# Falling output tiles sent whole to a row buffer in device memory and reversed there by later transfers

## The chip, the cores and the metric

The kernel runs on one core of a Trainium2 chip. The metric is device time in microseconds of one execution. Before the change it is 1046.65 us, the median of three runs (1045.64 to 1047.59).

The core has a matrix engine (TensorE, PE in the profile; PEld are its weight loads), a vector engine (VectorE, DVE), a scalar engine (ScalarE, ACT), a general engine (GpSimd, POOL) and a sync engine (SyncE, SP). Here SP issues nearly all transfers. Each engine takes its instructions in the order in which they were written and waits on semaphores for the others. 16 DMA engines carry the transfers.

## The reference

```python
# q, k, v: (4, 8, 768, 64); block 32
scores = q @ k.T / sqrt(64)                      # per batch and head
mask = neighbours | first, last block row/column | 3 sampled blocks per block row
attn = softmax(where(mask, scores, -1e9))
x = (attn @ v) heads side by side                # (4, 768, 512)
mixed = real(fft(fft(x, axis=1), axis=2))
u = x + mixed
un = (u - mean(u)) / sqrt(var(u) + 1e-6)
out = u + maximum(un @ w_ch1, 0) @ w_ch2         # 512 -> 2048 -> 512
```

## The kernel before

**Tiles.** The 768 rows (tokens) of a batch lie in six tiles of 128 partitions, three in `xA` (tiles 0, 1, 2) and three in `xB` (tiles 3, 4, 5), each 512 columns of 4 bytes, so a row is 2 KB. The order of rows in the tiles is not that of the tensor: it is chosen so that the Fourier transform can fold row s with row 768 - s. `_ORDER` (L53) lists it as (tile, first partition, runs, jump between runs, rows of a run, first row, step). In tiles 0, 1 and 5 the rows rise in steps of 2. In tiles 2, 3 and 4 they **fall** in steps of 2: partition 0 holds one row, partitions 1 to 63 and 64 to 126 two falling runs that interleave in the tensor, and partition 127 the last row. `_rows` (L81) turns this into access patterns; for a falling tile that is one transfer of one row, one of 126 rows (runs of 63, outermost dimension 2) and one of one row.

**Stages.** `slot` (L1566) is the attention for two units of 128 keys x 384 queries x 2 heads; there are 96 slots, 24 to a batch. In a slot PE makes scores (L583), ScalarE takes their exponential (L603, or L611 in place), VectorE applies the mask (L613), GpSimd or VectorE adds up (L643, L638), and PE multiplies by the values (L657). The scores go to one of two buffers of PSUM, so PE's next scores wait until L613 or L603 has read the ones before. Two heads' output is transposed (L680) and copied by ScalarE into `x` (`place`, L681), or, for later pairs, reaches `x` through a row buffer in device memory (`place_blocks`, L696 and L700).

When a batch's attention is done, its `mixer` runs in the gaps of the next batch's slots: the Fourier transform (`fourier`), normalization (L946 to L960), a block transpose (L1019) written to a buffer `far` (L1020), read back as `unT` (L1032, four loads of 192 KB for each half), differences of unT (L1070), the hidden layer by a scheme with seven products for eight (`quad`, L1116, sums L1121, relu L1125), and the output layer (`channels`, L1281; L1284 adds it into `x`). After the last of four rounds `channels` calls `store`, tile by tile: xA's in the order 2, 0, 1, then xB's 3, 4, 5.

**What sets the order.** All is written out ahead by a planner in Python that keeps a clock for each engine (`when`) and puts mixer steps (`apart`, `late`) into gaps (`gap`, `until`). Transfers have no place in its clocks: SP issues them in the written order. `x` has two buffers for each half, so batch b + 2 writes over batch b. `slot` therefore runs the rest of batch b's mixer (`until`, L1629 and L1644) before it places the first pair of batch b + 2, and the copy L681 waits for the transfers that read the old `x`. The last batch (`last`) has its own output scheme (`outputs`, L1349, L1356) with stores in halves.

Of the kernel before, what the change touches and what calls it, by code (L numbers as in the profile page):

```python
# [11 lines left out]
FP32 = mybir.dt.float32  # L12
# [10 lines left out]
def _words(ap, n):  # L23

    return bass.DRamTensorHandle(ap.tensor.name, (2 * n,), I32)
# [15 lines left out]
def _grid(ap, start, runs, jump, n, step):  # L41
# [17 lines left out]


_TURNED = (((0, 0, (128, 64, 2), (64, 128, 2), (1, 1, 64)),
# [19 lines left out]
def _rows(view, tile):  # L81

    got = []
    for t, p0, runs, jump, n, s0, step in _ORDER:
        if t != tile:
            continue
        at = view[s0:s0 + 1, :]
        row, col = list(at.ap[0])[0], list(at.ap[1])
        if jump > 0 > step:
            got.append((p0, runs * n, bass.AP(tensor=at.tensor, offset=at.offset,  # L90
                                              ap=[[jump * row, runs], [step * row, n], col])))
            continue
        for r in range(runs):
            at = view[s0 + r * jump:s0 + r * jump + 1, :]
            got.append((p0 + r * n, n, bass.AP(tensor=at.tensor, offset=at.offset,
                                               ap=[[step * row, n], col])))
    return got
# [3 lines left out]
def kernel(  # L101
# [14 lines left out]
    nc = tc.nc  # L116

    B, H, S, D = q.shape
    DM = H * D
    FF = w_ch1.shape[1]  # L120
    P = 128
# [9 lines left out]
    T = C // 2  # L131
# [55 lines left out]
    far_p = ctx.enter_context(tc.tile_pool(name="far_p", bufs=1, space=bass.MemoryType.DRAM))  # L187
# [114 lines left out]
    def bit(n):  # L302
# [5 lines left out]
                      in_=bass.AP(tensor=_words(sampled_blocks, NB * NR), offset=0,  # L308
                                  ap=[[0, NB], [1, 2 * NB * NR]]))
# [138 lines left out]
    for w, w_sb in ((w_ch1, w1_sb), (w_ch2, w2_sb)):  # L448
        rows, cols = w.shape
        words = _words(w, rows * cols)  # L450
        for row in range(rows // P):
            for col in range(0, cols, WN):
                src = bass.AP(tensor=words, offset=2 * (row * P * cols + col),
                              ap=[[2 * cols, P], [1, 2 * WN]])
# [527 lines left out]
    z_at = [0.0, 0.0]  # L982
    rstd_at = deque()
    finished = set()
    folded = set()

    def mixer(b, xA, xB):
# [56 lines left out]
        t, s = {}, {}  # L1044
# [243 lines left out]

        def store(half, m, cols=slice(0, DM), queue=nc.sync):
            x = (xA, xB)[half]  # L1290
            for p0, cnt, rows in _rows(out[b][:, cols], T * half + m):
                queue.dma_start(out=rows, in_=x[p0:p0 + cnt, m, cols])
            if cols.stop == DM:
                stored[half] += 1
            if stored[half] == T:
                finished.add((b, half))

        stored = [0, 0]
        last = b == B - 1
# [127 lines left out]
        for r in range(0 if last else NF // 4):  # L1430
# [21 lines left out]
    needed = set()  # L1452
    state = {"paired": False, "total": None, "w": 0, "got": 0, "owed": 0.0, "ready": 0.0,
             "back": 0.0, "place": None,
             "alone": False, "drain": lambda: None}

    def channel_step():
        masks["by_pe"] = False
        late.popleft()[0]()
# [61 lines left out]
    def until(met, alone=False):  # L1521

        state["alone"] = alone
        while not met():
            if late:
                channel_step()
                soon = state.pop("soon", None)
                gap(2.0, start=soon)
            else:
                do_apart()  # L1530
        state["alone"] = False
# [24 lines left out]
    def w_loads():  # L1556
        while state["got"] < min(len(wchunks), state["w"] + len(W_ROOMS)):
            w_load(state["got"])
            state["got"] += 1

    def w_steps(sl):
        while state["w"] < min(len(wchunks), W_PACE * sl):
            w_round(state["w"])
            state["w"] += 1

    def slot(sl):  # L1566
        phase, r = divmod(sl, SB)
        n, s = divmod(sl, SP)
        units = range(SLOT * sl, SLOT * sl + SLOT)
# [55 lines left out]
        if s >= ((4 if late else 5) if reuse else 3) and (n, 0) in oT_at and once(n):  # L1625
            b, j = pairs[n]
            at = oT_at[n, 0]
# [12 lines left out]
        if sl < B * SB and n % NP == 1 and s == 1:  # L1640
            b = pairs[n - 1][0]
            at = oT_at[n - 1, 1]
            if b >= 2:
                until(lambda: (b - 2, 1) in finished)  # L1644
                at = when["PE"] + LEAVES
# [46 lines left out]
        while short and (not more or soon) and (  # L1692
# [5 lines left out]
            short.remove(item)  # L1698
            item[2]()
        w_loads()  # L1700
        w_steps(sl)
        table_step(sl)

# [32 lines left out]
    begin(B - 1)  # L1736
    state["drain"] = lambda: None
    until(lambda: len(finished) == 2 * B, True)
    ordered.close()

    def general():
        qA = tp_p.tile([P, S], FP32, tag="qT", name="qA")
        kA = tp_p.tile([P, S], FP32, tag="kT", name="kA")
        spread_q(qA[D:KA, :], maskT)
        spread_k(kA[D:KA, :], ident[0:NB, 0:NB])
        for b in range(B):
            xs = [xp.tile([P, T, DM], FP32, tag=tag, name="x") for tag in ("xA", "xB")]
            for h in range(H):  # L1750
                qt = ld.tile([P, C, 2, D], FP32, tag="q", name="qg")
                for t in range(C):
                    for p0, cnt, rows in _rows(q[b, h], t):
                        nc.sync.dma_start(out=qt[p0:p0 + cnt, t, 0, :], in_=rows)
                nc.sync.dma_start(out=qt[:, :, 1, :],
                                  in_=k[b, h].rearrange("(p c) d -> p c d", p=P))
                vt = ldv.tile([P, C, D], FP32, tag="v", name="vg")
                nc.sync.dma_start(out=vt, in_=v[b, h].rearrange("(p c) d -> p c d", p=P))
                for half in range(2):
                    tp = ps_t.tile([P, HS], FP32, tag="t", name="tpg")  # L1760
                    for c in range(3):
                        nc.tensor.transpose(tp[:, c * P:(c + 1) * P],
                                            qt[:, 3 * half + c, :, :], ident)
                    sl = slice(half * HS, (half + 1) * HS)
                    nc.vector.tensor_scalar(out=qA[0:D, sl], in0=tp[0:D, :], scalar1=scale,
                                            scalar2=None, op0=ALU.mult)
                    nc.vector.tensor_copy(out=kA[0:D, sl], in_=tp[D:2 * D, :])
                op = ps_o.tile([P, C, D], FP32, tag="o", name="og")
                rs = sm.tile([P, C, 1], FP32, tag="r", name="rs", bufs=2)
                for t in range(C):  # L1770
                    s = ps_s.tile([P, 2, 512], FP32, tag="s", name="sg")
                    for half in range(2):
                        nc.tensor.matmul(s[:, half, 0:HS], qA[0:KA, t * P:(t + 1) * P],
                                         kA[0:KA, half * HS:(half + 1) * HS],
                                         start=True, stop=True)
                    nm = sm.tile([P, 1], FP32, tag="nm", name="nm")
                    nc.vector.tensor_reduce(out=nm, in_=s[:, :, 0:HS], axis=AX.XY, op=ALU.max,
                                            negate=True)
                    e = ep.tile([P, 2, HS], FP32, tag="e", name="eg")
                    nc.scalar.activation(out=e, in_=s[:, :, 0:HS], func=ACT.Exp, bias=nm,  # L1780
                                         scale=1.0, accum_out=rs[:, t, :])
                    eT = ep.tile([P, C, P], FP32, tag="e", name="eT")
                    for half in range(2):
                        tp = ps_t.tile([P, 3, P], FP32, tag="t", name="etp")
                        for c in range(3):
                            nc.tensor.transpose(tp[:, c, :], e[:, half, c * P:(c + 1) * P],
                                                ident)
                        nc.vector.tensor_copy(out=eT[:, 3 * half:3 * half + 3, :], in_=tp)
                    for c in range(C):
                        nc.tensor.matmul(op[:, t, :], eT[:, c, :], vt[:, c, :],  # L1790
                                         start=(c == 0), stop=(c == C - 1))
                nc.vector.tensor_scalar(out=rs, in0=rs, scalar1=1e-9, scalar2=None, op0=ALU.add)
                nc.vector.reciprocal(out=rs, in_=rs)
                for half, x in enumerate(xs):
                    sl = slice(half * T, half * T + T)
                    nc.vector.tensor_tensor(out=x[:, :, h * D:(h + 1) * D], in0=op[:, sl, :],
                                            in1=rs[:, sl, :].broadcast_to([P, T, D]),
                                            op=ALU.mult)
            before, after, rest = mixer(b, *xs)
            for step in before + after:  # L1800
                step[1]()
            for fn, _ in rest:
                fn()

    with tc.If(over > 0):
        general()
# [37 lines left out]
```

## Time and profile before

| | |
|---|---|
| median of three runs | 1046.65 us |
| the profiled execution | 1045.29 us |
| its span, first to last instruction | 1043.6 us |
| granted TensorE clock, mean | 0.994 |
| DMA | 58.06 MB, mean 56 GB/s |
| packets | 163582, of these under 512 B 144298 |
| output stores | 75 transfers, 71 from SP and 4 from ScalarE |

The busy time of an engine is its share of the span; transfers are counted by queue. In a timeline row stand the start and the duration in us, the engine, the line of the kernel, the operation, the tile written and the tile read, how many instructions were merged into the row, and in brackets how long the engine had been idle and what ended that. A waits row gives the total, the number and the longest of one kind of wait. "SPq" is SP's queue of issues; a duration there is the time to issue, not the time to land.

### The profile page before, as it was taken

The numbers are of one execution on the slowest core, as the hardware profiler recorded it, in microseconds if no ns is written. First come the engines' busy times: TensorE is split into PE (matmuls) and PEld (weight loads), VectorE is DVE, ScalarE is ACT, GpSimd is POOL, SyncE is SP. The second block draws the span as 40 slices with busy tenths as digits, with TensorE's granted clock in tenths as the row PEclk, the third lists the DMA queues.
The fourth block names the chain that finished last, engine by engine and source line by source line (L and its number), as shares of the span: only waits on it lengthen the run. The fifth ranks groups of instructions, "written<-read, shape, count | busy, mean of one in ns | idle before, by whom it ended". The sixth has DMA issues, their size and how long they took to land.

```text
span 1043.6 us, 12498 instructions
## 1 busy us (share of the span) xinstructions
PE 1018.6 (98%) x4382; PEld 537.0 (51%) x4382; DVE 683.2 (65%) x1246; ACT 359.3 (34%) x727; POOL 257.7 (25%) x287
## 2 busy tenths in 40 slices
PE   8999999999999999999999998999999999999996
PEld 4444345435565454444535653444444764578575
DVE  6899895978745646655677367665458475674663
ACT  6998765563021012433341111253220221210210
POOL 1000173662000203545560003256540221000000
PEclk9999999999999999999999999899999999999998
DMA  7767422291000143322320005521010001000001
GB/s 213 225 190 234 99 47 46 51 153 25 1 1 20 41 58 65 73 47 45 63 46 1 1 20 101 91 48 43 17 23 8 0 1 42 20 0 1 1 19 45
DMA packets 163582, 58.06 MB, mean 56 GB/s; under 512 B 144298, under 2 KB 154296, under 8 KB 163512
## 3 DMA queue, kind: packets, MB, share of 16 engines
q1 hardware_dynamic: 162216, 56.46, 24.1%
q10 hardware_dynamic: 1264, 0.72, 0.3%
q8 instruction: 36, 0.59, 0.2%
q14 instruction: 34, 0.28, 0.1%
q0 software_dynamic: 32, 0.01, 0.0%
HBM read 43.80 MB, written 13.37 MB: 55 GB/s over the span
## 4 chain that ended last, share of the span: by engine, by line
PE 84%; DVE 8%; DMA 2%; ACT 2%; SPq 2%; issue 1%; ACTq 0%; DVEq 0%
PE y L1281 20%; PE z L1116 16%; PE s L583 11%; PE o L657 9%; PE yp L1116 8%; PE yy L1349 7%; PE xp L1116 4%; PE zp L865 2%; PE sp L728 1%; PE s L593 1%; DMA far<-un 1%; ACT e L603 1%; DVE t L1070 1%; PE yz L1224 1%; DVE acc L638 1%
## 5 line engine op out<-in xcount | busy, mean ns | idle before, releaser
L643 POOL TENSOR_TENSOR acc<-acc,e 128x384 f32<-128x384 f32 x160 | 163.4, 1054 | 126.3 <-DVE e L613 106.7
L583 PE MATMUL s<-qT,kT 64*128 64x384 f32 x768 | 154.5, 518 | 9.5 <-DVE e L613 5.4
L657 PE MATMUL o<-e,vr 128*64 128x384 f32 x768 | 141.7, 497 | 0.0
L1281 PE MATMUL y<-w_sb,hB 128*128 128x512 f32 x264 | 118.9, 601 | 0.0
L1281 PE MATMUL y<-w_sb,hA 128*128 128x512 f32 x264 | 117.1, 595 | 0.0
L613 DVE TENSOR_TENSOR e<-s,mask 128x768 f32<-128x768 f32 x86 | 78.3, 950 | 53.9 <-ACT s L611 45.9
L583 PEld LDWEIGHTS s<-qT,kT 64*128 64x128 f32 x768 | 64.4, 187 | 90.0 <-ACT e L603 22.7
L1284 DVE TENSOR_TENSOR x<-y,x 128x512 f32<-128x512 f32 x66 | 45.6, 691 | 98.3 <-PE y L1281 98.1
L611 ACT ACTIVATE s<-s 128x768 f32<-128x768 f32 x86 | 65.1, 791 | 107.3 <-PE s L583 107.2
L603 ACT ACTIVATE e<-s 128x768 f32<-128x768 f32 x106 | 81.0, 814 | 54.2 <-PE s L593 32.9
L643 POOL TENSOR_TENSOR acc<-e 128x384 f32<-128x384 f32 x42 | 48.7, 1180 | 201.5 <-ACT e L603 121.9
L1116 PE MATMUL z<-unT,t 128*128 128x384 f32 x256 | 93.1, 486 | 0.0
L657 PEld LDWEIGHTS o<-e,vr 128*64 128x64 f32 x768 | 47.9, 136 | 69.4 <-issue 67.0
L1281 PEld LDWEIGHTS y<-w_sb,hB 128*128 128x128 f32 x264 | 49.6, 192 | 62.0 <-issue 61.3
L1121 DVE TENSOR_TENSOR hA<-z,hA 128x384 f32<-128x384 f32 x64 | 35.7, 557 | 69.8 <-PE z L1116 69.7
L1281 PEld LDWEIGHTS y<-w_sb,hA 128*128 128x128 f32 x264 | 49.2, 190 | 59.5 <-issue 55.7
L1125 ACT ACTIVATE hA<-hA 128x384 f32<-128x384 f32 x64 | 33.5, 523 | 121.8 <-DVE hA L1121 121.8
L1116 PEld LDWEIGHTS z<-unT,t 128*128 128x128 f32 x256 | 48.6, 190 | 34.1 <-DVE hA L1121 0.4
L1125 ACT ACTIVATE hB<-hB 128x384 f32<-128x384 f32 x64 | 33.5, 523 | 86.0 <-DVE hB L1121 86.0
L1136 ACT COPY hA<-xp 128x384 f32<-128x384 f32 x32 | 15.3, 477 | 129.3 <-PE xp L1116 129.3
L1116 PE MATMUL z<-t,w_sb 128*128 128x384 f32 x128 | 46.7, 487 | 1.5 <-DVE t L1070 1.5
L1116 PE MATMUL xp<-unT,w_sb 128*128 128x384 f32 x128 | 47.2, 492 | 0.0
(236 smaller groups left out, 1440.4 us busy)
## 6 DMA issues: line engine op xcount, KB each, us to landing
wraw<-in_moe_w_ch_dram SPq DMA_DIRECT2D x32, 512.0 KB
vr<-in_v_dram SPq DMA_DIRECT2D x30, 192.0 KB
far<-un SPq DMA_DIRECT2D x18, 256.0 KB
unT<-far SPq DMA_DIRECT2D x24, 192.0 KB
qb<-in_q_dram SPq DMA_DIRECT2D x44, 96.0 KB
kb<-in_k_dram SPq DMA_DIRECT2D x44, 96.0 KB
out_dram<-x SPq DMA_DIRECT2D x11, 252.0 KB
out_dram<-x SPq DMA_DIRECT2D x19, 128.0 KB
```

The costliest lines, as they stand in the source:

```text
L583: nc.tensor.matmul(s[:, i, 0:HS], kT[rows, c * P:(c + 1) * P], qT[rows, queries], start=True, stop=u not in by_pe)
L603: nc.scalar.activation(out=e, in_=s[:, :, 0:HS], func=ACT.Exp, scale=scale)
L611: nc.scalar.activation(out=s[:, :, 0:HS], in_=s[:, :, 0:HS], func=ACT.Exp, scale=scale)
L613: nc.vector.tensor_tensor(out=e, in0=s[:, :, 0:HS], in1=m.broadcast_to([P, 2, HS]), op=ALU.mult)
L643: nc.gpsimd.tensor_add(out=acc[:, i, :], in0=start[:, i, :], in1=e[:, i, :])
L657: nc.tensor.matmul(o[D * i:D * i + D, :], vt[:, i, c, :], e[:, i, :], start=(c == 0), stop=(c == C - 1))
L1116: nc.tensor.matmul(to, a[:, k, :], c[:, k, :], start=(k == 0), stop=(k == ND // 2 - 1))
L1121: tt(out=to, in0=ps, in1=a, op=ALU.add)
L1125: nc.scalar.activation(out=h, in_=h, func=ACT.Relu)
L1281: nc.tensor.matmul(y, hs[0, half][:, l, m * P:(m + 1) * P], w2_sb[:, 4 * r + l, :], start=(l == 0), stop=(l == 3))
L1284: nc.vector.tensor_tensor(out=x[:, m, :], in0=y, in1=x[:, m, :], op=ALU.add)
L1349: nc.tensor.matmul(ps, a[:, k, :], c[k // 2][:, k % 2, :] if isinstance(c, list) else c[:, k, :], start=(k == 0), stop=(k == 3))
```

## The change

A falling tile of the first three batches is sent whole, 128 rows as they lie, to a buffer of device memory (`falls`, two buffers for each of the three tiles). For tiles 2 and 3 the store of partition 0's row stays as it was. The other rows are put in a list, `owed`, as two transfers for each tile, from the buffer to `out`: 63 or 64 falling rows each (64 rows for both of tile 4, whose first row joins its first run). Such a transfer has sixteen column parts of 32 elements (128 bytes) as its outermost dimension, then the rows. At the end of each slot, ahead of `w_steps`, one of them is issued if it comes from an earlier slot. What is left is issued ahead of the last batch's first store. The last batch's own stores are not changed. The written order of PE, ScalarE, VectorE and GpSimd has no part in it.

```diff
+_FALLS = {2: ((1, 63, 382), (64, 64, 383)), 3: ((1, 63, 766), (64, 64, 767)),
+          4: ((0, 64, 640), (64, 64, 639))}
...
         def store(half, m, cols=slice(0, DM), queue=nc.sync):
             x = (xA, xB)[half]
+            while owed and last:
+                owed.popleft()[1]()
+            falls = T * half + m in _FALLS and not last
+            if falls:
+                turn_round(T * half + m, x[:, m, :])
             for p0, cnt, rows in _rows(out[b][:, cols], T * half + m):
-                queue.dma_start(out=rows, in_=x[p0:p0 + cnt, m, cols])
+                if not falls or (p0 == 0 and _FALLS[T * half + m][0][0]):
+                    queue.dma_start(out=rows, in_=x[p0:p0 + cnt, m, cols])
...
+        def turn_round(t, x):
+
+            rows = far_p.tile([P, DM], FP32, tag=f"fall{t}", name="falls", bufs=2)
+            nc.sync.dma_start(out=rows, in_=x)
+
+            def fall(p0, n, s0):
+                at, to = rows[p0:p0 + 1, :], out[b][s0:s0 + 1, :]
+                w = DM // 16
+                nc.sync.dma_start(
+                    out=bass.AP(tensor=to.tensor, offset=to.offset,
+                                ap=[[w, 16], [-2 * DM, n], [1, w]]),
+                    in_=bass.AP(tensor=at.tensor, offset=at.offset,
+                                ap=[[w, 16], [DM, n], [1, w]]))
+
+            for run in _FALLS[t]:
+                owed.append((state["slot"], lambda run=run: fall(*run)))
...
     def slot(sl):
+        state["slot"] = sl
...
         w_loads()
+        if owed and owed[0][0] < sl:
+            owed.popleft()[1]()
         w_steps(sl)
```

More of the change, by code (lines that the diff above doesn't have):

```diff
@@ L984 @@
     finished = set()
+    owed = deque()
     folded = set()
@@ L1454 @@
              "back": 0.0, "place": None,
-             "alone": False, "drain": lambda: None}
+             "slot": 0, "alone": False, "drain": lambda: None}
     def channel_step():
@@ L1738 @@
     until(lambda: len(finished) == 2 * B, True)
+    assert not owed
     ordered.close()
@@ L1803, in general @@
                 fn()
+            while owed:
+                owed.popleft()[1]()
     with tc.If(over > 0):
```

## The prediction

> **What bounds the kernel now.** I read the page first, then the waits, then the timeline around the one long stop of TensorE, then the granted clock in short windows.
>
> ```profile
> span 1043.6 us, 12498 instructions
> PE 1018.6 (98%) x4382; PEld 537.0 (51%) x4382; DVE 683.2 (65%) x1246; ACT 359.3 (34%) x727; POOL 257.7 (25%) x287
> ACT x L681 <- DMA far<-un: 8.7, 1, 8.7
> ACT x L681 <- DMA out_dram<-x: 1.9, 1, 1.9
> PE s L583 <- DVE e L613: 5.4, 2, 4.5
> ```
>
> TensorE (PE) is busy for 98% of the span, so a change in transfers can give only what PE idles (25 us in all) or what the clock loses. The third column of a wait is the longest one: a single copy on ScalarE, the placing of attention output into x (L681), waits 8.7 us for a transfer, and PE waits once for 4.5 us. The timeline shows that these are one event, in the fourth batch's attention (us from the start, duration; "x" counts merged instructions, the bracket is idle time before):
>
> ```profile
> 633.06 1.53 SPq L1292 DMA_DIRECT2D out_dram<-x  x3
> 635.09 0.35 SPq L1020 DMA_DIRECT2D far<-un  x1
> 636.49 1.19 SPq L1292 DMA_DIRECT2D out_dram<-x  x2
> 637.79 0.53 SPq L1020 DMA_DIRECT2D far<-un  x1
> 641.98 3.96 SPq L1032 DMA_DIRECT2D unT<-far  x4
> 645.98 1.94 SPq L1292 DMA_DIRECT2D out_dram<-x  x2
> ...
> 646.00 2.80 PE L657 MATMUL o<-e,vr 128*64 128x384 f32 x16
> ...
> 650.26 0.48 ACT L681 COPY x<-xt 128x384 f32<-128x384 f32 x1 [8.70 <-DMA far<-un]
> 650.64 0.85 ACT L540 ACTIVATE kb<-kb 128x768 f32<-128x768 f32 x1
> ...
> 651.48 1.50 ACT L611 ACTIVATE s<-s 128x768 f32<-128x768 f32 x2
> 652.31 1.82 DVE L613 TENSOR_TENSOR e<-s,mask 128x768 f32<-128x768 f32 x2 [3.91 <-ACT s L611]
> ...
> 653.32 2.93 PE L583 MATMUL s<-qT,kT 64*128 64x384 f32 x8 [4.52 <-DVE e L613]
> ...
> 656.18 5.15 PE L1281 MATMUL y<-w_sb,hB 128*128 128x512 f32 x8
> ```
>
> L681 overwrites the x of the second batch, so it waits for that batch's three xA stores (633.06, 636.49, 645.98). The profile names far<-un, but L681 touches no such tile; queue semaphores are shared, and the last store is the transfer that ends there. Behind L681 on ScalarE stand the exponentials (L611), behind them the masks (L613), and PE's next scores need the bank that L613 frees: 3.06 us from L681 to PE (650.26 to 653.32). PE ran dry at 648.80 and stood 4.52 us.
>
> Why was the last store issued only at 645.98? SP issues in order, and the four unT<-far loads before it waited until 641.98 for far<-un. The first two of these rows of the chain of waits price that transfer (the third is for a rival below):
>
> ```profile
> 635.09 6.83 DMA far<-un
> 648.66 2.59 DMA far<-un
> ...
> 662.76 3.63 DMA kb<-in_k_dram
> ```
>
> The same 256 KB took 6.83 us from issue to landing just behind the store of tile 2, and 2.59 us elsewhere. That store is the falling one: 126 rows as two runs of 63 in one transfer.
>
> ```profile
> 637.00:641.00 4.00, 4.00 (x18) 1.72 (x17) 3.18 (x6) 0.94 (x2) 0.77 (x2) 1.00 0.82 217
> 641.00:643.00 2.00, 2.00 (x7) 0.93 (x6) 1.04 (x3) 0.56 (x1) 0.00 (x0) 1.00 0.12 47
> ...
> 660.00:660.90 0.90, 0.90 (x4) 0.27 (x2) 0.00 (x0) 0.00 (x0) 0.00 (x0) 1.00 0.13 36
> ```
>
> The last three columns are granted clock, busy share of the 16 DMA engines, and GB/s. A share of 0.12 to 0.13 is two engines of sixteen; it follows each falling store (tile 2 here, tile 3 at 660). At 36 to 47 GB/s, 252 KB take 5.5 to 7.2 us, and whatever is spread over all engines lands only after those two.
>
> **The change, part by part.**
>
> *Removed:* nine falling stores (tiles 2, 3, 4 of three batches) and their last-row stores. *Added in their place:* one whole-tile transfer, x to a row buffer, with the shape of far<-un: 256 KB, priced at 2.59 us to landing and 0.35 to 0.53 us of SP, against 1.53 us for the three issues now. Tile 4's first-row store goes too. L681 and all later users of x then wait for this transfer and not for the reversal.
>
> *The gain at 633 to 656.* With far<-un landing 2.59 us after 635.09, that is at 637.68, SP is held only by its own issue until 637.79 + 0.53 = 638.32. The unT<-far loads then start at 638.32 and not 641.98, **3.66 us** sooner, and the xA store behind them likewise. That is the upper end. The lower end: the engines were 0.82 busy from 637 to 641, and this load stays, so the unT pieces may not move before 641.0; they now move from 643.0 at the earliest (the window up to there has only the two engines), so at least **2.0 us** are gained. The waiting time at the engines is shorter than this, since far<-un itself starts sooner; I take **3.0 us**, between the ends, nearer to the issue rows that SP's order gives directly. L681 then runs at 647.3, PE resumes at 650.3, and 1.5 of the 4.52 us stay.
>
> *The clock.* After the stop PE's instructions are long: 2.93 us for eight score matmuls and 5.15 us for a y, against these:
>
> ```profile
> 644.51 1.56 PE L583 MATMUL s<-qT,kT 64*128 64x384 f32 x8
> ...
> 640.98 3.60 PE L1281 MATMUL y<-w_sb,hB 128*128 128x512 f32 x8
> ...
> 529.40:530.30 0.90, 0.07 (x1) 0.00 (x0) 0.90 (x2) 0.49 (x1) 0.16 (x1) 1.00 0.57 91
> ...
> 649.00:653.30 4.30, 0.00 (x0) 0.00 (x0) 0.99 (x2) 3.04 (x6) 0.00 (x0) 0.89 0.48 157
> 653.30:656.00 2.70, 2.68 (x8) 1.14 (x8) 0.91 (x2) 1.68 (x4) 0.00 (x0) 0.50 1.28 166
> ```
>
> Excess: (2.93 - 1.56) + (5.15 - 3.60) = 1.37 + 1.55 = **2.92 us**. In 649.0 to 653.3 the clock averages 0.89; at half clock that is 4.3 x 0.11 / 0.5 = 0.95 us, so it fell at 652.35, 3.55 us into the idleness. The stop of 0.83 us before 530.3 left it at 1.00. A rest of 1.5 us, or 2.5 at the lower end, should keep it full. So the whole 2.92 us go.
>
> *Sum at this place:* 3.0 + 2.92 = 5.9 us; bounds 2.0 + 2.92 = 4.9 and 4.52 + 2.92 = 7.4 (no rest at all).
>
> *What is late next.* The right-hand differences, before which PE stops again:
>
> ```profile
> 665.79 0.69 DVE L1284 TENSOR_TENSOR x<-y,x 128x512 f32<-128x512 f32 x1 [2.99 <-PE y L1281]
> 666.39 1.42 DVE L1070 TENSOR_TENSOR t<-unT 128x768 f32<-128x768 f32 x1
> 667.85 1.64 DVE L1070 TENSOR_TENSOR t<-unT,t 128x768 f32<-128x768 f32 x1
> ...
> 669.63 1.53 PE L1116 MATMUL z<-t,w_sb 128*128 128x384 f32 x4 [1.30 <-DVE t L1070]
> ```
>
> L1070 has no idle before it: VectorE comes from L1284, which waits for PE. This 1.30 us stop follows PE's own order and shifts with it; I cost it at nothing. After it PE is the bound (98% of the span), so the shift reaches the end.
>
> *The first batch's stores (390 to 418)* delay L681 there by 1.9 us. PE's waits of this kind (scores for L613) come to 5.4 us, 4.5 of them in the stop above; so at most 0.9 us can be had here. I take 0, since PE had other products queued. *The third batch's* x is not reused: nothing.
>
> *The reversals:* 18 transfers, memory to memory, 126 or 128 KB each in 128-byte pieces, one per later slot. The trace has none. Nearest rows:
>
> ```profile
> 655.00:657.00 2.00, 2.00 (x5) 0.60 (x4) 0.96 (x1) 1.50 (x2) 0.00 (x0) 0.50 1.44 140
> ...
> 433.30 2.63 SPq L696 DMA_DIRECT2D row<-oT  x4
> 437.52 2.50 SPq L700 DMA_DIRECT2D x<-row  x4
> ...
> 657.82 6.89 SPq L232 DMA_DIRECT2D kb<-in_k_dram  x4
> ...
> 691.56 2.29 SPq L232 DMA_DIRECT2D kb<-in_k_dram  x4
> L681 ACT COPY x<-xt x20: 472/479/570, 26.1 to 682.9; 128x384 f32<-128x384 f32 x20
> SPq L1292 <- DVE x L1356: 137.2, 6, 121.9
> ```
>
> Lower end: 128-byte reads at 140 GB/s, 128 KB in 0.9 us. Upper end: 192 KB of row<-oT, 128-byte writes to memory, were issued and landed by 437.52, 4.2 us, so 2.8 us a reversal. I take 2 us, with about 0.6 us of SP each (row<-oT: 2.63 / 4). In SP's order the first stands behind the second batch's tile 3 store, the second behind the four kb loads, the other four behind the vr loads; none precedes anything of the sum above. They delay kb, the xB stores and vr by at most 5.6 us, while the kb loads, 6.89 us now behind a clogged pair of engines and 2.29 elsewhere, give 4.6 back. The xB placing (the last L681, 682.9) comes 12 us after the last xB store lands (664.81 + 3.34 + 2.6 = 670.7). Slack covers them: cost 0, and without that cover 5.6 us. The third batch's six are flushed in the order ahead of the last batch's first store, so SP issues them at once after that batch's stores, in its 121.9 us of idleness.
>
> [...]
>
> **Rivals.**
> 1. *The wait moves to L1070.* In the chain of waits a kb load lands at 666.4 (662.76 + 3.63), just where L1070 starts; L1070 reads unT and not kb, so the name may again stand for a shared semaphore. If unT's second half really lands only then, it moves 3.0 us sooner with SP's order, while PE comes 5.9 sooner: 2.9 us are lost again, gain 3.0, **1043.7 us**. Against: no idle before L1070.
> 2. *Half of the way.* Only 0.9 us or less is gained because another transfer holds unT<-far; PE still rests over 3.55 us and the clock falls: **1045.8 us**.
> 3. *It doesn't do what it says:* the buffer transfer also runs on few engines, or L681 waits for the row as before: **1046.7 us**. Against: far<-un has its shape.
> 4. *Slower: the reversals clog.* Two stand in SP's order ahead of the last xB stores. These have 12 + 4.6 = 16.6 us of slack to L681. From 8.3 us each on, L681 waits again and PE with it, 1 us for 1 us, and beyond 3.55 us the clock falls. At 14 us each: 28 - 16.6 = 11.4 us of stop and 2.9 of clock, less 5.9: **1055 us**. Against: five times the row<-oT price.
>
> **How the numbers follow.** The profiled execution took 1045.29 us (1043.6 and 1.7 around it); the median shown is 1046.65, 1.36 above. 1045.29 - 5.9 = 1039.4 on the one scale, **1040.7 us** on the other. Its own range, 4.9 to 7.4 us of gain and 1 us of scatter of the shown runs, is 1038.2 to 1042.8. Chances: forecast 0.66, rival 1 0.11, rival 2 0.06, rival 3 0.06, rival 4 0.11. The range 1037.6 to 1046.0 leaves out rival 4 and most of rival 3. A measurement can tell 0.2% (2.1 us) from no change: faster 0.77, same 0.12, slower 0.11.
>
> **What would show it.** Right: L681 near 647 with an idle of about 5 us or less before it; PE's stop before the scores under 2.5 us; clock 1.00 right after; kb's four issues near 2.3 us; no window at share 0.13. Wrong: L681 still near 650; a stop before L1070 or a later L681; windows in which reversals hold all engines for over 5 us.

## The result, and the profile after the change

The changed kernel takes 1041.90 us, the median of eight runs (1040.81 to 1043.65), and the kernel before 1045.77 us in eight runs beside it (1044.88 to 1047.59). The ratio is 0.9961, 95% interval 0.995 to 0.9972: **faster by 3.9 us**, and the interval stays clear of no change. The forecast was 1040.7 us and a gain of 5.9 us. The profiled execution took 1040.81 us, the shortest of the eight; its span is 1039.0 us, its mean granted clock 0.998.

The same views as before, in the same order. First the page's head and two rows of the waits (total, number, longest):

```profile
span 1039.0 us, 12502 instructions
PE 1016.1 (98%) x4382; PEld 536.0 (52%) x4382; DVE 683.2 (66%) x1246; ACT 359.4 (35%) x727; POOL 257.8 (25%) x287
ACT x L685 <- DMA far<-un: 5.8, 1, 5.8
PE s L587 <- DVE e L617: 2.4, 2, 1.6
```

The placing into x (L681 before, now L685) waits 5.8 us and not 8.7, and PE's longest wait for scores is 1.6 us and not 4.5. PE has the same 4382 matmuls with 2.5 us less busy time: work that ran at half clock before. The timeline of the same place in the changed kernel:

```profile
633.20 0.32 SPq L1315 DMA_DIRECT2D falls<-x  x1
635.23 0.32 SPq L1025 DMA_DIRECT2D far<-un  x1
...
638.59 4.13 SPq L1037 DMA_DIRECT2D unT<-far  x4
642.77 2.03 SPq L1303 DMA_DIRECT2D out_dram<-x  x2
647.46 0.48 ACT L685 COPY x<-xt 128x384 f32<-128x384 f32 x1 [5.75 <-DMA far<-un]
650.52 1.78 PE L587 MATMUL s<-qT,kT 64*128 64x384 f32 x8 [1.58 <-DVE e L617]
652.23 3.70 PE L1286 MATMUL y<-w_sb,hB 128*128 128x512 f32 x8
655.07 2.72 SPq L236 DMA_DIRECT2D kb<-in_k_dram  x4
663.93 2.18 SPq L1320 DMA_DIRECT2D out_dram<-falls  x3
664.22 1.53 PE L1121 MATMUL z<-t,w_sb 128*128 128x384 f32 x4 [1.30 <-DVE t L1075]
```

Read it against the rows of before. The buffer transfer (L1315) is one issue where there were three. The store of tile 2 and the far<-un behind it start 0.14 us later than before (633.20 for 633.06, 635.23 for 635.09): executions differ in when they reach this place, from 632.13 to 633.63 in the fourteen profiles, so a comparison of two profiles has to count from there. But SP reaches the unT<-far loads at 638.59 and not 641.98, so the plain store behind them goes out at 642.77 and not 645.98. L685 runs 2.80 us sooner and PE resumes 2.80 us sooner, 2.94 counted from the store of tile 2, and PE's stop is 1.58 us and not 4.52. The y behind it takes 3.70 us and not 5.15. The 1.30 us stop before z is the same to the hundredth, 5.41 us sooner (664.22 for 669.63). The windows of the changed kernel (last three columns: granted clock, share of the DMA engines, GB/s):

```profile
641.00:643.00 2.00, 2.00 (x8) 1.04 (x7) 1.97 (x4) 0.70 (x1) 0.00 (x0) 1.00 1.18 158
...
650.50:656.00 5.50, 5.48 (x20) 2.19 (x24) 3.57 (x5) 2.47 (x5) 0.00 (x0) 1.00 1.43 159
...
666.00:668.00 2.00, 2.00 (x8) 1.21 (x7) 1.86 (x4) 0.52 (x1) 0.00 (x0) 1.00 0.95 149
```

From 641 to 643, where the share was 0.12, it is now 1.18. (The share adds up the times of all packets over sixteen engines, so packets that overlap can bring it above 1; here the trace has up to 29 packets in flight at once.) The clock stays at 1.00 behind the stop. From 666 to 668 reversals hold the engines.

The 5.41 us do not all arrive. VectorE's last sum, before and then after, in the timeline:

```profile
1035.50 0.42 DVE L1356 TENSOR_TENSOR x<-yy,x 128x256 f32<-128x256 f32 x1 [0.97 <-PE yy L1349]
```

```profile
1030.10 0.42 DVE L1384 TENSOR_TENSOR x<-yy,x 128x256 f32<-128x256 f32 x1 [0.97 <-PE yy L1377]
```

It is 5.40 us sooner, but the span is only 4.6 us shorter (1043.6 to 1039.0): what follows the last sum, the last batch's last stores, which the change doesn't touch, took 0.8 us more.

### The profile page after: what moved, and what is told of

Same layout as the page of the kernel before. It is cut to its first block, busy times and chain, and to the rows that moved or that the text cites. A ratio compares the mean times of both kernels' runs of the same rounds, so it can differ in the third digit from the quotient of the medians.

```text
span 1039.0 us, 12502 instructions
## 1 busy us (share of the span) xinstructions
PE 1016.1 (98%) x4382; PEld 536.0 (52%) x4382; DVE 683.2 (66%) x1246; ACT 359.4 (35%) x727; POOL 257.8 (25%) x287
## 4 chain that ended last, share of the span: by engine, by line
PE 83%; DVE 8%; ACT 3%; DMA 2%; issue 2%; SPq 1%; ACTq 0%; DVEq 0%
PE y L1286 21%; PE z L1121 16%; PE s L587 10%; PE o L661 9%; PE yp L1121 8%; PE yy L1377 7%; PE xp L1121 4%; PE zp L869 2%; ACT e L607 1%; PE s L597 1%; PE sp L732 1%; DVE t L1075 1%; PE yz L1229 1%; DVE acc L642 1%; PE xt L684 1%
```

## The experiments

Eleven more kernels and the changed one again, each compared with runs of the kernel before on the same chip. Theory: tile 2's falling store, on two engines, holds the transfer behind it, which holds SP and with it the plain store that L681 waits for; PE's stop and the clock's fall follow from that. Rival readings: it is tiles 3 and 4, or the store's number or size and not its engines; or the clock has a cause of its own; or the reversals' place matters.

### Which tile

**Tile 2 alone (e4)** and **tiles 3 and 4 alone (e5)** leave the rest of the change out:

```diff
-_FALLS = {2: ((1, 63, 382), (64, 64, 383)), 3: ((1, 63, 766), (64, 64, 767)),
-          4: ((0, 64, 640), (64, 64, 639))}
+_FALLS = {2: ((1, 63, 382), (64, 64, 383))}
```

```diff
-_FALLS = {2: ((1, 63, 382), (64, 64, 383)), 3: ((1, 63, 766), (64, 64, 767)),
+_FALLS = {3: ((1, 63, 766), (64, 64, 767)),
```

> The changed kernel with only tile 2 sent through the buffer; tiles 3 and 4 are stored as before. Theory (all of the gain comes from the wait of L685 for xA in the second batch's stores): L685 near 647.5, stop 1.6 us, time 3.9 us below the kernel before (within 0.7), although the kb loads behind tile 3 take about 6.9 us again. Rival (SP's relief behind tiles 3 and 4 matters too): 1 us or more of the gain is missing.

> The changed kernel with only tiles 3 and 4 through the buffer; tile 2 as before. Theory: the kb loads take about 2.5 us, but L685 still waits until about 650, the stop stays 4.5 us and the clock falls: the time is that of the kernel before within 0.7 us. Rival: a part of the gain, 1 us or more, is here.

Tile 2 alone: 1040.83 us, ratio 0.9949 (0.9935 to 0.9962). Tiles 3 and 4 alone: 1046.31 us, 1.0005 (0.9996 to 1.0014). The timeline of e4, then of e5:

```profile
638.18 3.93 SPq L1036 DMA_DIRECT2D unT<-far  x4
...
650.07 1.78 PE L586 MATMUL s<-qT,kT 64*128 64x384 f32 x8 [1.54 <-DVE e L616]
...
655.37 6.84 SPq L235 DMA_DIRECT2D kb<-in_k_dram  x4
```

```profile
650.64 0.48 ACT L685 COPY x<-xt 128x384 f32<-128x384 f32 x1 [9.11 <-DMA out_dram<-x]
653.70 2.93 PE L587 MATMUL s<-qT,kT 64*128 64x384 f32 x8 [4.92 <-DVE e L617]
657.59 2.67 SPq L236 DMA_DIRECT2D kb<-in_k_dram  x4
```

The whole gain is tile 2's; by medians tile 2 alone is even 1 us below the changed kernel (1041.90), which is taken up under "What of the gain is missing". Tiles 3 and 4 take SP's four kb issues from 6.84 to 2.67 us, 4.2 us of the queue's time, and none of it shows in the time: nothing late stands behind them. In e5 the row names the wait rightly, too: the last plain store (out_dram<-x), where the row of before says far<-un.

### Is it the number of engines

**The buffer transfer in two blocks (e3)** was to put the same bytes on two engines again:

```diff
-            nc.sync.dma_start(out=rows, in_=x)
+            of = rows[0:1, :]
+            nc.sync.dma_start(out=bass.AP(tensor=of.tensor, offset=of.offset,
+                                          ap=[[64 * DM, 2], [DM, 64], [1, DM]]), in_=x)
```

> The changed kernel, but the whole-tile transfer into the row buffer is written with an outermost dimension of 2 (two blocks of 64 rows), so that it runs on few engines; bytes, order and the later reversals stay. Theory (the store's place on two engines is the cost): a share near 0.13 comes back after it, the copy L685 waits until about 650, TensorE stops about 4.5 us, the clock falls, and the time is that of the kernel before within 1 us. Rival (what helps is that the reversal is put off, or that SP has fewer issues there): L685 stays near 647.5 and the time 3.9 us below the kernel before.

1042.75 us, 0.9963 (0.995 to 0.9977), with a stop of 1.60 us: the changed kernel once more. The two blocks lie one behind the other, so they are a single run of 128 rows, and SP reaches the unT<-far loads at 638.29 (638.59 in the changed kernel, 641.98 before): this outermost 2 bound nothing. That something merges the two blocks is a reading; no run shows where. The experiment missed its aim and counts as a repeat. **Two interleaved blocks (e9)** do not make a single run; the reversal's addresses are adapted:

```diff
-            nc.sync.dma_start(out=rows, in_=x)
+            of = rows[0:1, :]
+            nc.sync.dma_start(out=bass.AP(tensor=of.tensor, offset=of.offset,
+                                          ap=[[DM, 2], [2 * DM, 64], [1, DM]]), in_=x)
...
-                at, to = rows[p0:p0 + 1, :], out[b][s0:s0 + 1, :]
+                i = 2 * (p0 % 64) + p0 // 64
+                at, to = rows[i:i + 1, :], out[b][s0:s0 + 1, :]
...
-                                ap=[[w, 16], [DM, n], [1, w]]))
+                                ap=[[w, 16], [2 * DM, n], [1, w]]))
```

> The changed kernel, with the whole tile written into the row buffer as two blocks of 64 rows that interleave (outermost dimension 2, which can't be merged into one run as the plain blocks of the first try were), and the reversals read it in that order; out is the same. Theory (engines): windows at a share near 0.13 come back behind the buffer transfer, far<-un lands near 641.9, L685 waits until about 650, TensorE stops about 4.5 us, the clock falls: the time is that of the kernel before within 1 us. Rival (putting off the reversal is what helps): L685 near 647.5 and 3.9 us below the kernel before.

1046.75 us, 1.0009 (1.0 to 1.0018), beside 1045.25 for the kernel before: the gain is gone. Timeline and windows of e9:

```profile
642.30 3.91 SPq L1037 DMA_DIRECT2D unT<-far  x4
653.55 2.88 PE L587 MATMUL s<-qT,kT 64*128 64x384 f32 x8 [4.18 <-DVE e L617]
658.22 6.83 SPq L236 DMA_DIRECT2D kb<-in_k_dram  x4
```

```profile
641.20:642.20 1.00, 1.00 (x7) 0.73 (x6) 0.47 (x1) 0.93 (x2) 0.00 (x0) 1.00 0.13 49
653.50:657.00 3.50, 3.45 (x9) 1.59 (x10) 1.77 (x2) 2.24 (x5) 0.00 (x0) 0.52 1.35 163
```

Still one issue, still 256 KB in whole rows, still reversed later; only the outermost dimension is 2. The unT loads start at 642.30, the stop is back at 4.18 us, the clock at 0.52, the kb issues at 6.83 us. The shares of 0.12 in before and 0.13 here agree: in before's trace 2.00 packets are in flight on average from 641 to 643, and 0.13 of sixteen engines is 2.1. It is the number of engines. What is shown is this outermost 2 in two transfers, the falling store and the interleaved buffer transfer; other sizes were not tried.

### The clock by itself

**Filler in the stop (e6)** puts fifteen matmuls of the identity, read by nobody, ahead of the late scores in the kernel before:

```diff
     def slot(sl):
...
+        if sl == 79:
+            warm(15)
```

> The kernel before, with 15 matmuls of the identity (about 3.2 us at full clock), whose result nobody reads, ahead of the scores of slot 79, where TensorE stands. Transfers and waits stay. Theory (the long scores and y after the stop are the lowered clock, worth 2.9 us): the clock stays at 1.00, the scores start again near 653.3 and take 1.6 us, the y 3.7 us, and the time is 2.9 us below the kernel before. Rival (they are long because of something else there, such as the transfers): they stay at 2.9 and 5.2 us and the time at that of the kernel before.

1043.66 us, 0.9986 (0.9977 to 0.9995). In its timeline L681 and the late scores come as late as ever, yet what follows is short:

```profile
649.29 3.62 PE L319 MATMUL warm<-ident 128*128 128x128 f32 x30
650.99 0.48 ACT L681 COPY x<-xt 128x384 f32<-128x384 f32 x1 [8.87 <-DMA far<-un]
654.05 1.78 PE L583 MATMUL s<-qT,kT 64*128 64x384 f32 x8 [1.15 <-DVE e L613]
655.76 3.70 PE L1281 MATMUL y<-w_sb,hB 128*128 128x512 f32 x8
```

Scores 1.78 us for 2.93 and y 3.70 for 5.15: **2.60 us that hang on the clock alone** and not on transfers. By medians 1.8 us arrive (1045.44 to 1043.66). So stop and clock are two terms, and they add.

### The reversals

**At once (e7)** issues tile 2's reversals right behind the buffer transfer:

```diff
-                owed.append((state["slot"], lambda run=run: fall(*run)))
+                fall(*run)
```

> The changed kernel, with the two reversals of a tile issued right behind its buffer transfer and not in later slots. Theory (they have to stay out of SP's order there): SP waits about 2 us for the buffer transfer to land and issues two more transfers, far<-un and the four unT loads come 1.3 us or more later, L685 runs near 649, TensorE stops about 3 us, and the time is 1.5 to 2 us above the changed kernel. Rival (only the release of x counts, and the reversals may stand anywhere): the time of the changed kernel within 0.5 us.

1043.54 us, 0.9983 (0.9974 to 0.9991), about half of the gain. Timeline and windows of e7:

```profile
634.83 1.30 SPq L1320 DMA_DIRECT2D out_dram<-falls  x2
639.63 3.98 SPq L1037 DMA_DIRECT2D unT<-far  x4
651.35 2.51 PE L587 MATMUL s<-qT,kT 64*128 64x384 f32 x8 [2.78 <-DVE e L617]
653.79 4.46 PE L1286 MATMUL y<-w_sb,hB 128*128 128x512 f32 x8
```

```profile
648.53:651.94 3.41, 0.63 (x6) 0.30 (x4) 1.61 (x2) 3.41 (x8) 0.00 (x0) 1.00 0.38 68
651.94:655.35 3.41, 3.41 (x8) 1.34 (x7) 1.72 (x3) 1.86 (x3) 0.00 (x0) 0.50 1.45 152
```

The reversals stand in SP's order ahead of far<-un, so unT loads start 1.04 us later than in the changed kernel (1.41 counted from the buffer transfer) and the stop grows by 1.20 us. The stop of 2.78 us **cost the clock as well**: 0.50 from 651.94, scores 0.73 us and y 0.76 us longer. The fall comes 0.59 us after PE has resumed; the section on the missing gain comes back to this. By the medians, putting the reversals off is worth 1.6 us (1043.54 - 1041.90).

**Half the piece (e10)**, 32 column parts of 64 bytes:

```diff
-                w = DM // 16
+                w = DM // 32
...
-                                ap=[[w, 16], [-2 * DM, n], [1, w]]),
+                                ap=[[w, 32], [-2 * DM, n], [1, w]]),
...
-                                ap=[[w, 16], [DM, n], [1, w]]))
+                                ap=[[w, 32], [DM, n], [1, w]]))
```

> The changed kernel, with thirty-two column parts of 64 bytes in the reversals in place of sixteen of 128, so twice the pieces for the same bytes. Theory (the reversals lie beside other work with several slots of slack): the DMA engines are busier where they run, and the time is that of the changed kernel within 0.5 us. Rival (they cost something in the slots where they run): 1 us or more above it.

1041.57 us, 0.996 (0.9947 to 0.9972): as the changed kernel. Timeline and window of e10 (the window to compare is the changed kernel's at 666):

```profile
663.62 3.59 SPq L1320 DMA_DIRECT2D out_dram<-falls  x3
```

```profile
666.00:668.00 2.00, 2.00 (x8) 1.21 (x7) 1.56 (x4) 0.52 (x1) 0.00 (x0) 1.00 0.91 88
```

The engines move 88 GB/s there and not 149, and SP needs 3.59 us for three issues in a row and not 2.18 (a single one, at 654 or 658, takes 0.58 us in both kernels). Nobody waits for either: reversals that take SP 1.65 times as long are still covered.

### What of the gain is missing

**The changed kernel again** gave 1041.71 us, 0.9959 (0.9946 to 0.9973), beside 1045.25 for the kernel before, so the 3.9 us stand.

> The changed kernel once more, beside the others on one chip: 3.9 us below the kernel before, with runs 1 us apart according to whether the clock falls near 884 and how long the last stores take.

In two of the experiments' profiles (e3 and e4, 0.53 and 0.56 from 884 to 887.5) the clock fell once more near 884, behind two short pauses of PE among transposes. The pauses in the changed kernel's timeline, two windows of e3 (it has the same pauses), and windows of the changed kernel:

```profile
882.25 0.66 PE L1006 MATMUL utp<-ident,un 128*128 128x128 f32 x4 [1.16 <-DVE un L964]
883.64 0.63 PE L1006 MATMUL utp<-ident,un 128*128 128x128 f32 x4 [0.73 <-ACT unT L1007]
```

```profile
880.79:884.20 3.41, 1.52 (x11) 1.16 (x11) 2.52 (x6) 1.46 (x4) 0.97 (x2) 1.00 0.42 96
884.00:887.50 3.50, 3.50 (x7) 1.86 (x7) 3.33 (x7) 1.07 (x2) 0.00 (x0) 0.53 0.99 155
```

```profile
881.31:884.72 3.41, 1.73 (x10) 1.30 (x11) 2.52 (x6) 1.46 (x3) 0.97 (x2) 1.00 0.49 108
884.00:887.50 3.50, 3.31 (x13) 1.77 (x12) 3.43 (x8) 1.06 (x2) 0.00 (x0) 1.00 0.91 145
```

Why the same pauses cost the clock in one profile and not in another can be worked out from the traces. A trace records when the clock changes. In before it rises at 7.20 us, falls 645.12 us later (652.32), rises again after 6.83 us and falls 378.88 us after that (1038.02). In the changed kernel it rises at 7.50 us and falls 1027.41 us later, at its end. These lengths are 189, 2, 111 and 301 times 3.413 us. In e7 the half clock lasts one such length (the window from 651.94 to 655.35), and the windows of e3 and e4 add up to about 3.4 us (0.53 from 884 to 887.5 and 0.99 to 892; 0.98 from 876 to 884 and 0.56 to 887.5). So in these traces the clock changes at the ends of stretches of 3.41 us whose place differs from one execution to the next. Counted in these stretches, PE idled for 100% (before), about 97% (e9, with the fall near 653.64 that the 0.52 of its window gives), 81% (e7) and 55% (e3: 1.52 us busy of 3.41) ahead of a fall in mid-kernel; in before and the changed kernel no stretch at full clock with a smaller idle share ended in one (the largest were 34% in before at 884.43 and 49% in the changed kernel at 881.31).

**The pauses filled (e13)**: identity matmuls between the transposes of the last batch, five in the first pause and three in the second (`warm(n)` makes n of them).

```diff
             un = uns.pop((half, m))
+            if half == 1 and m != 1:
+                warm(5 if m else 3)
```

> The changed kernel with matmuls of the identity, whose result nobody reads, put in PE's order behind the later halves of the falling flips of the last batch, five before tile 0 and three or so elsewhere, so that the two pauses of 1.16 and 0.73 us near 881 to 887 are filled. Theory (the clock falls near 884 in part of the runs for about 3.4 us, which costs 1.1 us there, because PE pauses twice): with the pauses filled the granted clock is 1.00 in 884 to 887.5 of the profile, the mean clock of nearly every run is 0.997 or 0.998, and the median is 0.5 to 1 us below the changed kernel's 1041.7, near 1041.0. Rival: the fall in part of the runs isn't set by these pauses, or the filler takes as much as it saves: 1041.7 or above, with the same spread of mean clocks from 0.995 to 0.998.

1041.75 us, 0.9968 (0.9957 to 0.9979), runs from 1040.71 to 1043.45. The pauses are gone, the clock is 1.00 in the profile's window, and six of seven runs have a mean clock of 0.997 or 0.998; in two sets of the changed kernel that was six of thirteen. Yet median and spread are what they were: runs at 0.998 alone go from 1040.7 to 1042.3. So the theory falls: the fall near 884 is real where a profile shows it, but it is not what parts the median from the profiled execution.

**The end of the kernel.** From the end of VectorE's last sum to the end of the span it is 7.64 to 8.02 us in the six kernels that send no tile or only some tiles through the buffers (before, e4, e5, e6, e12, e14), and 8.46 to 10.02 us in all eight profiles with all nine (the changed kernel twice, e3, e7, e9, e10, e11, e13): 1.5 us more on average. The larger part, 0.9 us on average, stands in one issue of SP, a store of 64 rows of the last batch just ahead of the last sum. SP's timeline there in before, in the changed kernel and in the changed kernel again:

```profile
1035.33 0.48 SPq L1292 DMA_DIRECT2D out_dram<-x  x1
```

```profile
1029.93 0.65 SPq L1303 DMA_DIRECT2D out_dram<-x  x1
```

```profile
1029.84 1.98 SPq L1303 DMA_DIRECT2D out_dram<-x  x1
```

It takes 0.48 or 0.49 us in each of the six kernels, 0.64 or 0.65 in three of the eight profiles (changed kernel, e7, e13) and 1.57 to 2.39 in the other five, and the last falling store is issued behind it. So about 1.5 of the 5.5 us gained at the stop are lost again here. That leaves 4.0, near the 3.9 us of the medians; the two profiles of the changed kernel (1040.81 and 1042.15 us) differ by 1.34 us, their ends by 1.39. Tile 2 alone (e4) has the gain without this loss (7.78 us). Why that issue is slower when all nine tiles go through the buffers is not shown.

### The order instead of the buffers

If the plain store is late only because it stands in SP's order behind four loads that wait, it can be issued ahead of them. In the code a flip is the step that transposes one tile and writes it to `far`, and `fetch(0)` issues the four unT loads. **The changed kernel with the third batch's first unT loads one far<-un later (e11)**, **the kernel before with the same edit and nothing else (e12)**, and **e12 with e13's filler (e14)**:

```diff
-            if half == 1 and len(late) < 2 * T:
+            if half == 1 and len(late) < 2 * T and (b < 2 or m != 1):
                 fetch(0)
```

> The changed kernel, with unT's first four loads of the third batch issued one far<-un later, so that the store of tile 1 stands ahead of them in SP's order (the other engines' instructions are the same). Theory (what holds L685 now is SP's order, four loads of 4.1 us): the store is issued near 640.1 and L685 runs near 643, the stop of 1.6 us is gone, and the time is 1.6 us below the changed kernel. Rival (unT comes too late for L1075): the stop of 1.3 us before z grows by what the first one loses, and the time is that of the changed kernel.

> The kernel before, without row buffers, with the same one step in SP's order. Theory (the falling store on two engines hurts through SP's order alone): the store of tile 1 is issued near 640.1 in place of 645.98, L681 runs near 643.5, TensorE does not stop and the clock stays: up to 7.4 us below the kernel before, more than the change under study gives. Rival 1 (the two clogged engines hold every transfer behind them): the store lands with the falling one and L681 runs after 645. Rival 2: far<-un and unT are late for L1070, and a part of the gain is lost there.

> The kernel before, with unT's first loads of that one flip a step later (the plain store first, 1038.9 us by itself) and the same filler in the last batch's pauses. Theory as above: 1038.0 to 1038.6, clock 1.00 in 880 to 890 and mean clocks of the runs near 0.998. Rival: 1038.9 or a little above, the filler only takes place. Either way the plain store reaches its landing near 641 to 642 and the stop before the scores stays under 1 us.

| | median us | ratio to before |
|---|---|---|
| e11, on the changed kernel | 1039.69 | 0.994 (0.9927 to 0.9954) |
| e12, on the kernel before | **1038.93** | 0.9937 (0.9924 to 0.9951) |
| e14, e12 with filler | 1039.06 | 0.9939 (0.9925 to 0.9952) |

PE's late scores in e11 (no idle before them), then the timeline of e12:

```profile
648.96 1.56 PE L587 MATMUL s<-qT,kT 64*128 64x384 f32 x8
```

```profile
639.00 1.16 SPq L1292 DMA_DIRECT2D out_dram<-x  x2
641.08 4.45 SPq L1032 DMA_DIRECT2D unT<-far  x4
643.06 0.48 ACT L681 COPY x<-xt 128x384 f32<-128x384 f32 x1 [2.43 <-DMA far<-un]
...
648.41 1.78 PE L583 MATMUL s<-qT,kT 64*128 64x384 f32 x8 [0.55 <-DVE e L613]
...
656.33 6.89 SPq L232 DMA_DIRECT2D kb<-in_k_dram  x4
```

In e12 the slow store is still there (the kb issues take 6.89 us, as before), but the plain store leaves at 639.00 and not 645.98, L681 runs 7.20 us sooner than before (6.27 counted from the store of tile 2: this execution was 0.93 us ahead there), and 0.55 us of the stop is left. So the plain store landed in time although it was issued behind the falling one, which refutes e12's first rival. One moved issue beats both kernels, 6.3 us under the kernel before beside it. Filler on top (e14) adds nothing. e11 against e12 is not told apart by their intervals, so beside this edit the row buffers bring nothing measurable. By the profiles e11 is 0.84 us faster from the store of tile 2 to the stop before z (29.15 and 29.99 us) and loses 1.68 us behind the last sum (9.55 and 7.87).

## Why the prediction was right

**The bound and the chain** held. The store that L681 waits for, SP held by the unT loads, these held by a transfer behind a store on two engines: e9 brings all of it back by that one dimension, e4 shows that tile 2 suffices, and e12 that the wait was in SP's order. Two of its signs came out a little long, L685's idle (5.75 us for about 5) and kb's issues (2.72 us for 2.3).

**The buffer transfer at full width, 3.0 us (2.0 to 3.66).** The stop went from 4.52 to 1.58 us: 2.94. Counted from the store of tile 2, SP reached the unT loads 3.53 us sooner, near the upper end; 0.59 us of that did not reach L685 (2.94). That the engines, at a share of 1.18 from 641 to 643, are the next limit was the reason for a value between the ends; it fits, but no run tests it. That 3.0 was met to 0.06 us is luck: it was chosen between the ends and not worked out, and in the changed kernel's second profile the stop is 1.10 us.

**The clock, 2.92 us.** Measured 1.15 (scores, 2.93 to 1.78) + 1.45 (y, 5.15 to 3.70) = 2.60. The step took as full speed the scores' 1.56 us and y's 3.60; in this place they take 1.78 and 3.70 in the changed kernel at clock 1.00, and the same in e6 and e12. The scores' 1.56 comes back in e11, where PE did not stop; the y takes 3.70 there too, so its 0.10 us are not the stop's. Of the bounds of this step one was unsafe: a rest of 2.5 us, it said, should keep the clock full. e7's 2.78 us did not. The lower end of the sum could then have been below 4.9; the taken value, a rest of 1.5 us, was on the safe side. Nor were the 3.55 us read from before a length that a stop must have: they were the time to the end of a stretch. Nor was the stretch (3.41 us) ahead of a fall always idle throughout: 81% of it in e7 and 55% in e3.

**The sum, 5.9 us.** 2.94 + 2.60 = 5.54, and counted from the store of tile 2 PE's own rows show 5.55 at z (5.41 and the 0.14 of the later start) and VectorE's last sum 5.54. The sum at this place was right within half a microsecond. **"The shift reaches the end"** is the step that was wrong in size: it put the loss behind PE at nothing, and in the changed kernel's two profiles the time behind the last sum is 0.8 and 2.2 us longer than before. That is why 3.9 us arrive by medians and not 5.5. The loss goes with having all nine tiles in the buffers; its cause is open, and e13 rules out the pauses near 884.

**No gain in the first and third batch** is borne out by e4, which changes tile 2 in all three batches and has its gain in the one stop, and by e5.

**The stop before z shifts with PE** held: 1.30 us before and after, so the first rival falls.

**The reversals, 2 us each at no cost.** The 128-byte packets of three of them lie between 665.38 and 668.26: 0.96 us each. The lower end (0.9) was the better row, not row<-oT. SP's 0.6 us each came out at 0.58 for a single one and 0.73 for three in a row (2.18 / 3). The kb issues gave back 4.17 us (6.89 to 2.72; 4.6 forecast). That they cost nothing where they run holds: e10, with dearer reversals, is no slower. Against the fourth rival: reversals in 128-byte pieces run at 149 GB/s, in 64-byte pieces at 88, and neither held anything up. In these runs smaller pieces were slower, but not at a price that clogs.

**The other rivals.** The second (half-way, the clock still falls) is not the changed kernel, but e7 is of its kind, at 1043.54 us and not 1045.8. The third (the change doesn't do what it says) is e9: the gain is gone. That its 1046.75 us is the 1046.7 given is luck, as the kernel before took 1045.25 beside it.

## What to carry to other kernels

Where an engine waits for a store, look first at what stands ahead of that store in the issuing queue and what that waits for: here one issue moved ahead of four waiting loads gained more than the buffers and eighteen transfers that made the loads wait less. In this kernel a transfer whose outermost dimension of 2 interleaves left the engines at a share of 0.12 to 0.13, and a full-width transfer issued behind it landed late (6.83 us and not 2.59); but that cost time only at a place where somebody waits, here for one store of nine. A stop of TensorE as long as the one before is to be priced twice, once for itself (4.52 us) and once for the half clock behind it (2.60 us): in these runs stops up to 1.62 us left the clock alone, stops of 2.78 us and more did not, and in e3 pauses of 1.16 and 0.73 us close together were followed by a fall as well. And a shift has to be followed to the very end: about a quarter of this one was lost behind the last sum, where nothing had been changed.

## What the runs showed of the hardware that was not expected

- In before and the changed kernel the clock changed only at the ends of stretches of 3.41 us counted from its first rise (after 189, 191 and 302 of them, and after 301). It fell after a stop of 2.78 us (e7; 81% of the stretch idle), and in some executions after pauses of 1.16 and 0.73 us with transposes between (e3, 55%; not in the changed kernel, 49%).
- The first eight score matmuls behind even a short stop (0.55 us in e12) took 1.78 us, and 1.56 us without one; in the changed kernel, behind 1.58 us, they took 1.78 at clock 1.00.
- An outermost dimension of 2 whose blocks adjoin did not bind a transfer to two engines (e3: the unT<-far loads start at 638.29); interleaved, it did (e9: a share of 0.13, the loads at 642.30).
- Reversing memory to memory in 128-byte pieces ran at 149 GB/s with the engines at a share of 0.95, against the 217 GB/s at a share of 0.82 of 2 KB rows before.
- SP's issue of one and the same late store took 0.48 or 0.49 us in six kernels (0.48 in before) and 0.64 to 2.39 us in all eight profiles (0.65 and 1.98 in the changed kernel's two) with eighteen reversals far ahead of it.
